# A fused adaLN attention block on one core: key columns from scaled, unshifted rows, modulation one group ahead, gate spread by DMA

## The chip, the cores and the metric

The kernel runs on one NeuronCore of a Trainium2 chip. The metric is the device time of one execution in microseconds (us); a median over runs is given with its range. The profile of a run reports a *span*, from the first to the last instruction.

## The reference

```python
B, N, D = 2, 256, 1152
mod = (silu(c) @ w_mod).reshape(B, 6, 1, D)
shift_a, scale_a, gate_a = mod[:, 0], mod[:, 1], mod[:, 2]     # the other three are not used
h   = layernorm(x) * (1 + scale_a) + shift_a
q, k, v = split(h @ wqkv)                                      # each [B, N, D]
p   = softmax(q @ k^T * D**-0.5)
out = x + gate_a * ((p @ v) @ wo)
```

All tensors are bf16. One fact makes the change legal. The shift adds the same vector to every row of `h`, so it adds the same vector `s` to every key. A score then gets the extra term `q . s`, which is the same for all keys of one query, and softmax does not see it. Keys may therefore be made from rows without the shift; queries and values may not.

## The kernel before: what the argument touches

The 512 token rows are four tiles of 128 rows (tiles 0 and 1 are batch 0, tiles 2 and 3 batch 1). The 1152 features are nine rows of 128 (index `cc` or `k`). Each row tile is normalized, transposed on TensorE, and then scaled and shifted ("modulated") per feature, which gives `hT`. Scale and shift are computed on TensorE by matmuls with two moving columns, in four groups of features, as their weights arrive.

```python
GROUPS = [(0, 2), (2, 5), (5, 7), (7, 9)]
PASSES = [list(range(0, 7)), list(range(7, 14)), list(range(14, 18))]   # q: columns 0-8, k: 9-17

for g, (a, b_) in enumerate(GROUPS):          # loads, in this order, on one queue
    dma_mod(g)                                # scale weights, then shift weights of the group
    dma_wq(a, b_, 0, 7 * P, wkeys(0, a, b_))  # first seven projection columns
# ... then the other projection columns, the value columns, gate weights, wo

# first projection pass: seven accumulators, features outermost
for g, (a, b_) in enumerate(GROUPS):
    if g > 0:
        mod_mm(g, 1)                          # scale matmuls (128x2)
        mod_mm(g, 0)                          # shift matmuls
        mod_ev(g)                             # PSUM -> SBUF, VectorE
        for cc in range(a, b_):
            for b in range(B):
                modulate(cc, b, ...)          # hT = xnT * (1 + scale) + shift
    for k in range(a, b_):
        for j, bank in zip(PASSES[0], PASS1_BANKS):
            qk_mm(0, j, k, bank)              # 128x512 matmul, both batches
# ... two more passes, values, scores, softmax

# gate: one row of four times 288 columns, spread to 128 partitions by matmul
for k in range(DC):
    for j in range(4):
        ... matmul(ps[bank][32*j:32*(j+1), 0:GW], scT_sb[:, k, :], wgate_ap[...])
# ... copied to gaterow_sb; then, for each batch b and quarter j:
        ... matmul(ps[bank][:, 0:GW], sel_sb[:, 2*j + b, :], gaterow_sb[:, :])
        evac(...)                             # to gate_rep
# output tiles: ga = psum * gate_rep;  xo = x + ga;  DMA out
```

TensorE executes its matmuls in program order, so a matmul that waits holds back the matmuls behind it. `warm(n)` issues `n` matmuls of zeros whose result nobody reads, to keep TensorE active at the start.

Of the kernel before, what the change touches and what calls it, by code (L numbers as in the profile page):

```python
# [153 lines left out]
GROUPS = [(0, 2), (2, 5), (5, 7), (7, 9)]  # L154
PASSES = [list(range(0, 7)), list(range(7, 14)), list(range(14, 18))]
PASS1_BANKS = [5, 6, 0, 1, 2, 3, 4]
# [16 lines left out]
def _build(nc, es, x, c, wqkv, wo, w_mod, out):  # L173
# [25 lines left out]
    warm_sb = sb("warm_sb", [P, 512], bf16)  # L199
    c_sb = sb("c_sb", [2, D], bf16)  # L200
# [5 lines left out]
    mod_sb = sb("mod_sb", [P, 2, DC, 2], f32)  # L206
    gaterow_sb = sb("gaterow_sb", [P, GW], bf16)
    stat_sb = sb("stat_sb", [P, TT, 3, 6], f32)
    sums_sb = sb("sums_sb", [P, TT, 2], f32)
    nm2_sb = sb("nm2_sb", [P, TT], f32)  # L210
# [9 lines left out]
    sel_sb = sb("sel_sb", [P, 2 * 4, P], bf16)  # L220
# [7 lines left out]
    wm_off = {}  # L228
    off = 0
    for g, (a, b_) in enumerate(GROUPS):  # L230
        for kind in range(2):
            wm_off[(g, kind)] = off
            off += DC * (b_ - a) * P

    def wm_ap(g, kind):
        w = (GROUPS[g][1] - GROUPS[g][0]) * P
        return bass.AP(wm_sb, wm_off[(g, kind)], [[2 * DC * D, P], [w, DC], [1, w]])

    wgate_ap = bass.AP(wm_sb, 0, [[2 * DC * D, P], [D, DC], [1, D]])
    wo_ap = bass.AP(wm_sb, DC * D, [[2 * DC * D, P], [D, DC], [1, D]])  # L240

    def wm_keys(lo, hi):
        keys = []
        for (g, kind), o in wm_off.items():
            n = DC * (GROUPS[g][1] - GROUPS[g][0]) * P
            if o < hi and o + n > lo:
                keys.append(("wm", g, kind))
        return keys


    op(AC, lambda e: e.dma_start(c_sb[:, :], c[:, :]), w=[("c",)], dma=True)
    for i in range(TT):
        op(SP, lambda e, i=i: e.dma_start(x_sb[:, i, :], x_pi[:, i, :]), w=[("x", i)], dma=True)  # L253

    def dma_mod(g):
        a, b_ = GROUPS[g]
        for kind in (1, 0):
            base = kind * D
            op(SP, lambda e, g=g, kind=kind, lo=base + a * P, hi=base + b_ * P:
               e.dma_start(wm_ap(g, kind), wm_v[:, :, lo:hi]), w=[("wm", g, kind)], dma=True)  # L260

    def dma_wq(k0, k1, c0, c1, keys):
        op(SP, lambda e: e.dma_start(wq_sb[:, k0:k1, c0:c1], wq_v[:, k0:k1, c0:c1]),
           w=keys, dma=True)

    def wkeys(p, k0, k1):
        return [("w", p, k) for k in range(k0, k1)]

    for g, (a, b_) in enumerate(GROUPS):
        dma_mod(g)  # L270
        dma_wq(a, b_, 0, 7 * P, wkeys(0, a, b_))
    for k0 in range(0, DC, 3):
        dma_wq(k0, k0 + 3, 7 * P, 14 * P, wkeys(1, k0, k0 + 3))
    for k0 in range(0, DC, 3):
        dma_wq(k0, k0 + 3, 14 * P, 18 * P, wkeys(2, k0, k0 + 3))
    for k0 in range(0, DC, 3):
        dma_wq(k0, k0 + 3, 2 * D, 3 * D, wkeys(3, k0, k0 + 3))
# [7 lines left out]
    op(POOL, lambda g: g.memset(eps_sb[:, :], EPS_B), w=[("eps",)])  # L285
    op(POOL, lambda g: g.memset(scT_sb[:, :, :], 0.0), w=[("scT",)])
    op(POOL, lambda g: g.memset(sel_sb[:, :, :], 0.0), w=[("sel",)])
    for j in range(4):
        for b in range(2):
            op(POOL, lambda g, j=j, b=b: g.affine_select(  # L290
                out=sel_sb[:, 2 * j + b, :], in_=sel_sb[:, 2 * j + b, :],
                compare_op=ALU.not_equal, fill=1.0, base=-(32 * j + b),
                pattern=[[0, P]], channel_multiplier=1), r=[("sel",)], w=[("sel",)])

    def warm(n):
        for _ in range(n):
            op(PE, lambda pe: pe.matmul(ps[7][:, 0:512], warm_sb[:, 0:P], warm_sb[:, 0:512],  # L297
                                        start=True, stop=True),
               r=[("warm",)], w=[("ps", 7)])


    op(AC, lambda a: a.preload_act_table_set("natural_log_exp_and_others"))
    warm(4)

    def f_cT(pe):
        last = None
        for k in range(DC):
            last = pe.transpose(psb[6][:, 2 * k:2 * k + 2], c_sb[0:2, k * P:(k + 1) * P],
                                ident[0:2, 0:2])
        return last  # L310
    op(PE, f_cT, r=[("c",), ("ident",)], w=[("ps", 6)])
    cT_ps = psb[6][:, 0:2 * DC].rearrange("p (k b) -> p k b", b=2)
    op(DVE, lambda v: v.tensor_copy(cT_sb[:, :, :], cT_ps), r=[("ps", 6)], w=[("cT",)])
    op(AC, lambda a: a.activation(e1_sb[:, :, :], cT_sb[:, :, :], ACT.Exp, scale=-1.0),
       r=[("cT",)], w=[("e1",)])
    warm(8)


    def stats_dve(i):
        for q in range(3):  # L320
            op(DVE, lambda v, q=q: v.bn_stats(stat_sb[:, i, q, :], x_sb[:, i, q * 384:(q + 1) * 384]),
               r=[("x", i)], w=[("stat", i, q)])
        op(DVE, lambda v: v.bn_aggr(mv_sb[:, i, :], stat_sb[:, i, :, :]),
           r=[("stat", i, q) for q in range(3)], w=[("mean", i), ("var", i)])

    def sum_act(i):
        n = 0 if i == 1 else 2
        junk = qkT_sb[:, 3 * n:3 * n + 3, :].rearrange("p a t -> p (a t)")[:, 0:D]
        jk = [("qk", 3 * n + m) for m in range(3)]
        op(AC, lambda a: a.activation(junk, x_sb[:, i, :], ACT.Copy,  # L330
                                      accum_out=sums_sb[:, i, 0:1]),
           r=[("x", i)], w=jk + [("sum", i)])

    def sq_act(i):
        n = 1 if i == 1 else 3
        junk = qkT_sb[:, 3 * n:3 * n + 3, :].rearrange("p a t -> p (a t)")[:, 0:D]
        jk = [("qk", 3 * n + m) for m in range(3)]
        op(AC, lambda a: a.activation(junk, x_sb[:, i, :], ACT.Square,
                                      accum_out=sums_sb[:, i, 1:2]),
           r=[("x", i)], w=jk + [("sq", i)])  # L340

    def stats_act_end(i):
        op(DVE, lambda v: v.tensor_scalar(mv_sb[:, i, 0:1], sums_sb[:, i, 0:1], 1.0 / D, None,
                                          op0=ALU.mult), r=[("sum", i)], w=[("mean", i)])
        op(DVE, lambda v: v.scalar_tensor_tensor(nm2_sb[:, i:i + 1], sums_sb[:, i, 0:1],
                                                 -1.0 / (D * D), sums_sb[:, i, 0:1],
                                                 ALU.mult, ALU.mult),
           r=[("sum", i)], w=[("nm2", i)])
        op(DVE, lambda v: v.scalar_tensor_tensor(mv_sb[:, i, 1:2], sums_sb[:, i, 1:2],
                                                 1.0 / D, nm2_sb[:, i:i + 1],  # L350
                                                 ALU.mult, ALU.add),
           r=[("sq", i), ("nm2", i)], w=[("var", i)])

    def rstd(i):
        op(AC, lambda a: a.activation(lnv_sb[:, i:i + 1], mv_sb[:, i, 1:2], ACT.Ln,
                                      bias=eps_sb[:, 0:1], scale=1.0),
           r=[("var", i), ("eps",)], w=[("lnv", i)])
        op(AC, lambda a: a.activation(rstd_sb[:, i:i + 1], lnv_sb[:, i:i + 1], ACT.Exp, scale=-0.5),
           r=[("lnv", i)], w=[("rstd", i)])

    def xn(i):
        op(DVE, lambda v: v.tensor_scalar(xo_sb[:, i, :], x_sb[:, i, :], mv_sb[:, i, 0:1],  # L362
                                          rstd_sb[:, i:i + 1], op0=ALU.subtract, op1=ALU.mult),
           r=[("x", i), ("mean", i), ("rstd", i)], w=[("xo", i)])

    def xT(i):
        for cc in range(DC):
            bank, half = cc // 2, cc % 2
            op(PE, lambda pe, cc=cc, bank=bank, half=half: pe.transpose(  # L369
                psb[bank][:, half * T + i * P: half * T + (i + 1) * P],  # L370
                xo_sb[:, i, cc * P:(cc + 1) * P], ident[:, :]),
               r=[("xo", i), ("ident",)], w=[("ps", bank)])

    def xT_out(b, eng_of):
        for bank in range(5):
            n = 2 if bank < 4 else 1
            src = psb[bank][:, 0:n * T].rearrange("p (c t) -> p c t", c=n)[:, :, b * NTOK:(b + 1) * NTOK]
            dst = xnT_sb[:, 2 * bank:2 * bank + n, b * NTOK:(b + 1) * NTOK]
            keys = [("xnT", 2 * bank + h, b) for h in range(n)]
# [5 lines left out]

    def mod_mm(g, kind):
        a, b_ = GROUPS[g]
        w = (b_ - a) * P
        for cc in range(a, b_):
            col = (kind * DC + cc) * 2  # L390
            for k in range(DC):
# [278 lines left out]
```

## Time and profile before

| | before |
|---|---|
| runs quoted before the prediction | 110.34, 113.43, 113.9 us |
| all four runs of the first comparison | median 111.89 us (110.04 to 113.9) |
| profiled span | 110.1 us |
| TensorE busy | 99.1 us, 90% of the span |
| first projection matmul, first value matmul | 16.19 us, 61.6 us |

First the page of the kernel before: its span, TensorE's busy time, and three rows of the time slices (40 equal slices; a digit is the busy share in tenths, for PEclk the granted TensorE clock in tenths of full speed).

```profile
span 110.1 us, 1775 instructions
...
PE 99.1 (90%) x735; PEld 56.2 (51%) x735; DVE 43.9 (40%) x125; ACT 26.7 (24%) x61; POOL 4.2 (4%) x17
...
PE   5959459969969699999999999999999999999990
...
PEclk9999955785999999999999999999999999999999
DMA  3999999999999999996299400000000001112222
```

Counting slices from 0, TensorE is close to full from slice 6 on, with three dents (slices 8, 11 and 13); its clock is low in slices 5 to 9; the DMA engines are saturated in slices 1 to 17. To see which of these counts, look at the chain of work that ended last (columns: start us, length us, what):

```profile
3.06 8.22 DMA wm_sb<-in_w_mod_dram
...
16.19 5.29 PE psbank L459 x14
21.47 1.34 PE psbank L392 x54
22.81 0.02 issue
22.84 0.17 DVE mod_sb L401
23.00 0.08 DVE mod_sb L403
23.08 0.03 issue
23.11 0.61 DVE hT_sb L415 x2
23.72 0.05 issue
23.77 6.39 PE psbank L459 x21
...
37.04 24.73 PE psbank L459 x113
61.77 4.39 PE psbank L509 x27
...
86.98 0.49 PE psbank L601 x4
...
89.44 0.49 PE psbank L601 x4
89.93 17.08 PE psbank L620 x108
```

The last DMA wait of the chain ends at 11.28 us. From 16.19 us the chain is TensorE, except for the group starts: between 22.81 and 23.77 us TensorE waits while VectorE evicts scale and shift and modulates the first feature row. The same stop stands before the other two later groups (0.96 us each). Line 601 is the gate spread, 0.98 us. Note also the first 14 projection matmuls: 0.378 us each, while the 113 at 37 us took 0.219 each. The windows view says why (columns: stretch in us, length, TensorE busy, matmuls, granted clock, DMA share, GB/s):

```profile
core 0: us, PE busy (x), PEclk, DMA share, GB/s
16.20:20.40 4.20, 4.20 (x10) 0.50 1.11 334
20.50:23.80 3.30, 2.33 (x60) 1.00 1.14 316
23.90:27.20 3.30, 3.30 (x9) 0.50 1.18 295
27.30:61.60 34.30, 32.37 (x213) 1.00 0.95 340
```

TensorE had half its clock when the projections began, got full clock at 20.45 us, lost it again at 23.87 and had it back from 27.28 us. (A DMA share above 1 means that packets overlap.) Half-clock time inside the projection stream is 4.3 + 3.4 = 7.7 us, about 3.8 us lost.

### The profile page before, as it was taken

Reading aid. Unit: us, or ns where it says so; the run is one execution under the profiler, and the core shown is the slowest. Engines: PE = TensorE matmul, PEld = TensorE weight load, DVE = VectorE, ACT = ScalarE, POOL = GpSimd, SP = SyncE. Lnnn points to the kernel's source line nnn. Section 1 sums busy time; section 2 is a strip of 40 time slices with the busy share of each in tenths; the row PEclk is TensorE's granted clock in tenths of the full one; section 3 lists DMA queues with packets and bytes.
Section 4 is the critical chain, followed back from the end, with each engine's and each line's share of the span. In section 5 each row is a group of like instructions: output and inputs, shape, how many; then the busy total and the mean of one; then the engine's idle time right before and its main releaser. Section 6 shows DMA issues by size and latency. Waiting matters only on the chain.

```text
span 110.1 us, 1775 instructions
## 1 busy us (share of the span) xinstructions
PE 99.1 (90%) x735; PEld 56.2 (51%) x735; DVE 43.9 (40%) x125; ACT 26.7 (24%) x61; POOL 4.2 (4%) x17
## 2 busy tenths in 40 slices
PE   5959459969969699999999999999999999999990
PEld 1407333533445334444444568766666875655570
DVE  0798570040030380000800422643422785666672
ACT  4579230030020250000500415461111870000000
POOL 6610000000000000000000000000000000000000
PEclk9999955785999999999999999999999999999999
DMA  3999999999999999996299400000000001112222
GB/s 77 323 309 321 333 332 348 292 329 294 369 382 363 366 390 389 396 392 232 20 361 408 176 0 0 6 3 0 0 0 0 6 0 33 56 54 70 71 77 71
DMA packets 18956, 21.06 MB, mean 191 GB/s; under 512 B 770, under 2 KB 14978, under 8 KB 18948
## 3 DMA queue, kind: packets, MB, share of 16 engines
q1 hardware_dynamic: 18944, 20.94, 58.7%
q8 instruction: 6, 0.10, 0.4%
q14 instruction: 2, 0.02, 0.1%
q10 hardware_dynamic: 4, 0.00, 0.0%
HBM read 19.76 MB, written 1.18 MB: 190 GB/s over the span
## 4 chain that ended last, share of the span: by engine, by line
PE 81%; DMA 7%; DVE 6%; SPq 2%; issue 1%; ACT 0%
PE psbank L459 36%; PE psbank L509 16%; PE psbank L620 16%; DMA wm_sb<-in_w_mod_dram 7%; PE psbank L585 4%; PE psbank L522 4%; PE psbank L392 3%; DVE hT_sb L415 2%; SPq L253 2%; PE psbank L572 1%; DVE xnT_sb L381 1%; PE psbank L601 1%; DVE mod_sb L401 1%; DVE ga_sb L627 1%; DVE xo_sb L362 1%
## 5 line engine op out<-in xcount | busy, mean ns | idle before, releaser
L459 PE MATMUL psbank<-hT_sb,wq_sb 128*128 128x512 bf16 x162 | 39.6, 408 | 3.5 <-DVE hT_sb L415 3.5
L459 PEld LDWEIGHTS psbank<-hT_sb,wq_sb 128*128 128x128 bf16 x162 | 16.3, 104 | 25.4 <-issue 5.1
L509 PE MATMUL psbank<-wq_sb,hT_sb 128*128 128x384 bf16 x108 | 18.0, 326 | 0.0
L620 PE MATMUL psbank<-wm_sb,pvT_sb 128*128 128x384 bf16 (+2 forms) x117 | 17.7, 314 | 0.0
L620 PEld LDWEIGHTS psbank<-wm_sb,pvT_sb 128*128 128x128 bf16 x117 | 11.1, 98 | 6.6
L509 PEld LDWEIGHTS psbank<-wq_sb,hT_sb 128*128 128x128 bf16 x108 | 10.5, 98 | 6.9
L466 DVE CAST qkT_sb<-psbank 128x512 bf16<-128x512 f32 x10 | 6.3, 684 | 18.9 <-PE psbank L459 18.9
L468 ACT ACTIVATE qkT_sb<-psbank 128x512 bf16<-128x512 f32 x8 | 4.2, 597 | 21.2 <-PE psbank L459 21.2
L627 DVE TENSOR_TENSOR ga_sb<-psbank,gate_rep 128x384 bf16<-128x384 f32 (+2 forms) x13 | 6.8, 526 | 5.9 <-PE psbank L620 5.9
L297 PE MATMUL psbank<-warm_sb 128*128 128x512 bf16 x17 | 6.9, 556 | 1.2 <-DVE warm_sb L280 1.2
L401 DVE TENSOR_SCALAR mod_sb<-psbank 128x4 f32<-128x4 f32 (+1 forms) x4 | 0.7, 164 | 17.7 <-PE psbank L392 17.7
L417 ACT ACTIVATE hT_sb<-xnT_sb,mod_sb 128x256 bf16<-128x256 bf16 x4 | 2.3, 596 | 18.6 <-DVE mod_sb L403 18.6
L466 DVE CAST v_sb<-psbank 128x384 bf16<-128x384 f32 x6 | 3.2, 555 | 7.7 <-PE psbank L509 7.7
L369 PE MATMUL psbank<-ident,xo_sb 128*128 128x128 bf16 x36 | 3.1, 242 | 3.4 <-DVE xo_sb L362 3.4
L468 ACT ACTIVATE v_sb<-psbank 128x384 bf16<-128x384 f32 x6 | 2.9, 486 | 10.3 <-PE psbank L509 10.3
L392 PEld LDWEIGHTS psbank<-scT_sb,wm_sb 128*128 128x128 bf16 x162 | 4.7, 96 | 1.3 <-DMA wm_sb<-in_w_mod_dram 0.3
L392 PE MATMUL psbank<-scT_sb,wm_sb 128*128 128x2 bf16 x162 | 4.8, 164 | 0.2 <-DMA wm_sb<-in_w_mod_dram 0.2
L369 PEld LDWEIGHTS psbank<-ident,xo_sb 128*128 128x128 bf16 x36 | 2.5, 108 | 4.7 <-DVE xo_sb L362 4.5
L630 DVE TENSOR_TENSOR xo_sb<-x_sb,ga_sb 128x384 bf16<-128x384 bf16 (+2 forms) x13 | 4.5, 342 | 0.4
L585 PE MATMUL psbank<-pT_sb,v_sb 128*128 128x256 bf16 x36 | 4.3, 273 | 0.0
L522 PE MATMUL psbank<-qkT_sb 128*128 128x256 bf16 x36 | 4.1, 273 | 0.0
L415 DVE TENSOR_SCALAR hT_sb<-xnT_sb,mod_sb 128x256 bf16<-128x256 bf16 x14 | 4.0, 342 | 0.1
(57 smaller groups left out, 59.0 us busy)
## 6 DMA issues: line engine op xcount, KB each, us to landing
wm_sb<-in_w_mod_dram SPq DMA_DIRECT2D x6, 576.0 KB, 8.3
wq_sb<-in_wqkv_dram SPq DMA_DIRECT2D x4, 672.0 KB, 8.6
wq_sb<-in_wqkv_dram SPq DMA_DIRECT2D x3, 864.0 KB, 11.1
wm_sb<-in_w_mod_dram SPq DMA_DIRECT2D x1, 2592.0 KB, 17.8
wm_sb<-in_wo_dram SPq DMA_DIRECT2D x1, 2592.0 KB, 9.2
wm_sb<-in_w_mod_dram SPq DMA_DIRECT2D x2, 864.0 KB, 8.9
wq_sb<-in_wqkv_dram SPq DMA_DIRECT2D x3, 448.0 KB, 8.3
x_sb<-in_x_dram SPq DMA_DIRECT2D x4, 288.0 KB, 3.6
```

What stands on the lines that cost most here:

```text
L297: op(PE, lambda pe: pe.matmul(ps[7][:, 0:512], warm_sb[:, 0:P], warm_sb[:, 0:512], start=True, stop=True), r=[("warm",)], w=[("ps", 7)])
L369: op(PE, lambda pe, cc=cc, bank=bank, half=half: pe.transpose(psb[bank][:, half * T + i * P: half * T + (i + 1) * P], xo_sb[:, i, cc * P:( ...
L392: op(PE, lambda pe, cc=cc, k=k, col=col, src=wm_ap(g, kind), lo=(cc - a) * P: pe.matmul(ps[7][:, col:col + 2], src[:, k, lo:lo + P], scT_s ...
L415: op(DVE, lambda v: v.tensor_scalar(dst, src, sc, sh, op0=ALU.mult, op1=ALU.add), r=rk, w=wk)
L459: op(PE, lambda pe: pe.matmul(ps[bank][:, lo:hi], wq_sb[:, k, j * P:(j + 1) * P], hT_sb[:, k, lo:hi], start=(k == 0), stop=(k == DC - 1)), ...
L466: op(DVE, lambda v: v.tensor_copy(dst, src), r=r, w=w)
L468: op(AC, lambda a: a.activation(dst, src, ACT.Copy), r=r, w=w)
L509: op(PE, lambda pe, k=k, q=q, bank=bank: pe.matmul(ps[bank][:, 0:384], hT_sb[:, k, i * P:(i + 1) * P], wq_sb[:, k, 2 * D + q * 384:2 * D + ...
L522: op(PE, lambda pe, cc=cc: pe.matmul(ps[bank][:, 0:NTOK], qkT_sb[:, cc, i * P:(i + 1) * P], qkT_sb[:, DC + cc, b * NTOK:(b + 1) * NTOK], s ...
L585: op(PE, lambda pe, h=h, cc=cc, sbk=sbk: pe.matmul(ps[bank][:, h * NTOK:(h + 1) * NTOK], v_sb[:, 2 * b + sbk, cc * P:(cc + 1) * P], pT_sb[ ...
L620: op(PE, lambda pe, i=i, k=k, c0=c0, c1=c1, n=n, bank=bank: pe.matmul(ps[bank][:, 0:n], pvT_sb[:, k, i * P:(i + 1) * P], wo_ap[:, k, c0:c1 ...
L627: op(DVE, lambda v, b=b, c0=c0, c1=c1, n=n, bank=bank, s=s: v.tensor_tensor(ga_sb[:, s, 0:n], ps[bank][:, 0:n], gate_rep[:, b, c0:c1], ALU ...
```

## The change

There are five parts:

1. Key columns are made first, from scaled but unshifted rows (`h0T`). Scale weights are loaded first, in four groups. The shift weights come later and are added to `h0T` in a second pass, ahead of the query columns. Values use shifted rows.
2. A group's scale matmuls and scaling are issued one group ahead, behind the first seven matmuls of the group in progress. The shift is one group ahead likewise.
3. The work on row tiles is reordered at the start: a third of a tile's statistics goes to ScalarE, small arithmetic to GpSimd, and ten half-width matmuls of batch 0 (five key columns, two feature rows) start before batch 1's rows exist.
4. The gate row is computed earlier and spread by eight DMAs, not by matmuls.
5. GpSimd takes part of the scaling and shifting.

The edit also moves the idle matmuls: the kernel before has 4 and 8 of them at the start and 3 and 2 between the first transposes; the changed kernel has 5 and 9 at the start and none later.

The diff, cut to its core:

```diff
-GROUPS = [(0, 2), (2, 5), (5, 7), (7, 9)]
+SGROUPS = [(0, 2), (2, 4), (4, 6), (6, 9)]
+HGROUPS = [(0, 3), (3, 6), (6, 9)]
+NA = 7
+EARLY = 5
@@ loads
-    for g, (a, b_) in enumerate(GROUPS):
-        dma_mod(g)
-        dma_wq(a, b_, 0, 7 * P, wkeys(0, a, b_))
+    for g, (a, b_) in enumerate(SGROUPS):
+        load_s(g)                                   # scale weights
+        load_w("ka", a, b_, D, D + NA * P)          # seven key columns
+    load_h(0)                                       # shift weights
+    load_w("kb", 0, DC, D + NA * P, 2 * D)
+    for g, (a, b_) in enumerate(HGROUPS):
+        if g:
+            load_h(g)
+        load_w("qa", a, b_, 0, NA * P)
@@ start (cut: statistics, evictions)
+    for k in range(2):
+        for j in range(EARLY):
+            qk_mm("ka", h0T_sb, "pv", DC + j, k, j, b=0, start=(k == 0))
@@ first pass
-    for g, (a, b_) in enumerate(GROUPS):
-        if g > 0:
-            mod_mm(g, 1)
-            mod_mm(g, 0)
-            mod_ev(g)
-            for cc in range(a, b_): ...modulate...
-        for k in range(a, b_):
-            for j, bank in zip(PASSES[0], PASS1_BANKS):
-                qk_mm(0, j, k, bank)
+    for g in range(1, len(SGROUPS)):
+        a, b_ = SGROUPS[g]
+        for k in range(a, b_):
+            for j in range(NA):
+                qk_mm("ka", h0T_sb, "pv", DC + j, k, j)
+            if k == a and g + 1 < len(SGROUPS):
+                s_mm(g + 1)
+                scale_group(g + 1)
+            if k == DC - 2:
+                h_mm(0)
@@ gate
-            op(PE, lambda pe, ...: pe.matmul(ps[bank][:, 0:GW], sel_sb[:, 2 * j + b, :], gaterow_sb[:, :], ...
-            evac(AC if j % 2 == 0 else DVE, gate_rep[:, b, j * GW:(j + 1) * GW], ...
+            row = bass.AP(gaterow_sb, (32 * j + b) * GW, [[GW, 1], [0, P], [1, GW]])
+            op(SP, lambda e, ...: e.dma_start(gate_rep[:, b, j * GW:(j + 1) * GW], row), ...
```

## The prediction

> **What bounds it now.** Busy times by engine: TensorE works 99.1 of 110.1 us, 90%, and it ends 81% of the chain of waits. From the first projection matmul (16.19 us) to the last matmul (107.0) it is the pacemaker; DMA is saturated until about 51 us (330 to 390 GB/s in the slices), but the chain's last DMA wait ends at 11.28 us. So only TensorE time counts after 16 us. The chain, from 16.19 to the end of the q/k projections at 61.77 (45.6 us), holds:
> - 162 matmuls of 128x512: 35.4 us at full rate (113 of them took 24.73 us, 0.219 each);
> - 126 modulation matmuls: 3.1 us;
> - three stops before groups 2 to 4 (modulation evictions, then the first row): 0.96 us each, 2.9 us;
> - lost clock. The first 14 matmuls took 5.29 us, the next 21 took 6.39: 4.0 us over full rate. The granted clock reads 0.50 from 13.7 to 20.5 and from 23.9 to 27.3 us.
> The remaining 45.3 us of TensorE hold 0.98 us of gate broadcast matmuls.
>
> **What changes.**
> 1. Key columns use scaled, unshifted rows; softmax ignores the constant. So before a matmul only a scale is needed, and scales are computed a group ahead, while the previous group multiplies (7 matmuls, 1.5 us, against 0.17 + 2x0.3 on VectorE). I expect all three stops to go: -2.9 us. The modulation matmuls themselves stay.
> 2. The shift is a second pass over h (18 tile halves, 0.3 us each on VectorE, a third on GpSimd). It hides behind the two late key columns (18 x 0.219 = 3.9 us, against about 2.7 us of evictions and 0.6 us of shifts) and behind the query pass: 0.
> 3. Eight broadcast matmuls become DMAs issued after the gate row, more than 10 us before their use: -1.0 us.
> 4. Start. Ten half-width matmuls (batch 0, 1.1 us at full rate) run at about 11 to 13 us. But adding durations along each engine's order, row tile 3 is not sooner: its ScalarE third sits behind tile 2's rstd, which sits behind the scale eviction; its transpose waits for tile 1's evictions. I get batch 1's first matmul at about 17.5 us, 1.3 later than now. Net about +0.2.
> 5. Clock. The Trainium skill, "TensorE: Matmul & The Clock Gate", Part 1, says a free-running window of about 3.4 us of activity decides the clock. The trace agrees: its changes (6.85, 13.7, 20.5, 23.9, 27.3 us) lie on a grid of 3.41. Today the stop at 21.5 to 23.8 lets it fall again. The changed stream has no such stop, so one ramp remains, with 1.5 to 3.4 us lost by phase: about -1.6 against this trace. The two runs near 113.5 are, I think, worse phases (35 matmuls all at half clock lose 7.5 us, 3.5 more than here), so the median gains more.
>
> Sum: 110.1 - 2.9 - 1.0 + 0.2 - 1.6 = **about 105.0 us**, range 102.5 to 108.5. Chances: faster 0.90, same 0.07, slower 0.03.
>
> **What would show it.** Projections end near 56.5 instead of 61.8; no idle over 0.3 us before k/q matmuls after 20 us; one fall of the clock after the warm-up and one rise by 24.5; from the first value matmul to the end about 1 us shorter; less spread between runs. If step 4 is wrong, the first full-width matmul comes far from 19 us.
>
> **What would make it wrong.** GpSimd scales or shifts much slower than 0.5 us, or held up by VectorE; batch 1's rows later than 18.5 us; two extra falls of the clock; a weight load arriving late because keys' loads are reordered; gate copies delaying the outputs.

## The result, and the profile after

The changed kernel took 105.31 us (median of four runs, 104.89 to 106.4), the kernel before 111.89 us (110.04 to 113.9). The ratio is 0.9538, 95% interval 0.9451 to 0.9625. Ratios are the mean time of one kernel's fast runs over that of the other's of the same rounds, so they are not quite the ratio of the medians.

The page of the changed kernel, the same rows:

```profile
span 103.4 us, 1795 instructions
...
PE 94.3 (91%) x728; PEld 55.8 (54%) x734; DVE 44.8 (43%) x122; ACT 25.2 (24%) x64; POOL 8.7 (8%) x30
...
PE   5956458999999999999999999999999999999990
...
PEclk9999985579999999999999999999999999999999
DMA  2999999999999999999999400002777666764122
```

The three dents are gone. There is one low stretch of clock in place of two. The DMA row has something new: about 0.6 to 0.7 in slices 28 to 35, where before there was nothing until the outputs. Its chain (line 367 is the modulation matmuls, 419 the projections, 579 the values, 660 and 685 the attention output and `wo`):

```profile
3.16 5.87 DMA wm_sb<-in_w_mod_dram
...
13.98 1.20 PE psbank L349 x17
...
16.01 2.31 PE psbank L419 x10
18.32 0.22 issue
18.54 3.90 PE psbank L419 x10
22.44 0.43 PE psbank L367 x18
22.87 3.04 PE psbank L419 x14
...
55.86 4.55 PE psbank L579 x27
...
79.28 3.93 PE psbank L660 x36
83.20 17.08 PE psbank L685 x108
```

From 18.54 us there is no link on VectorE or GpSimd between TensorE's pieces: modulation matmuls (22.44) are followed at once by projections (22.87). The 0.22 us of "issue" before 18.54 is no stop but a lost record: the page lists 728 matmuls for 734 weight loads, one of these loads stands at 18.12 us without its matmul, and the full trace of after_again (734 of 734) has no such gap. The clock in windows:

```profile
core 0: us, PE busy (x), PEclk, DMA share, GB/s
10.50:14.80 4.30, 2.07 (x25) 1.00 1.13 325
15.00:21.60 6.60, 6.10 (x39) 0.50 1.08 347
21.80:55.80 34.00, 33.74 (x265) 1.00 1.08 366
```

The span fell by 6.7 us. The first value matmul came 5.75 us sooner (61.61 to 55.86 us), and from there to the end of the last `wo` matmul the time fell from 45.9 to 44.9 us. In the first part, the stops account for 2.9 us (2.90 to none), the ten early half-width matmuls for 1.1 us (five full ones at 0.2155 us each), the earlier first matmul of the stream for 0.2 us, and the clock for 1.0 us (half-clock time in the stream 7.7 to 5.7 us). That is 5.2 of 5.75 us; about 0.6 us is not itemised here.

Last, the new DMA work, from the view of the tile that the gate copies write:

```profile
L646 SPq DMA_DIRECT2D gate_rep<-gaterow_sb x8: 542/2264/3380, 70.4 to 84.4; - x8
...
DMA to landing us min/median/max: 5.4/8.7/11.1
```

Eight copies of only 72 KB each were issued over 14 us (the issue itself took up to 3.4 us), and each landed 5.4 to 11.1 us after it was issued. From the trace's landing times, the first four (batch 0) landed at 75.9 to 83.9 us and the others (batch 1) at 87.2 to 92.6 us; batch 0's gate is first used at 84.7 us. Together they moved 590 KB in 22.1 us, 27 GB/s, where the loads of the first half ran at over 300. The first output write could only be issued at 87.1 us, behind them on the same queue, and landed at 92.9 us. Nothing on the chain waited for this. The least slack was 3.6 us: the quarter of batch 1's gate that landed at 91.3 us is first read at 94.9 us.

### The profile page after: what moved, and what is told of

Read it like the earlier page. It is cut to its first block, busy times and chain, and to the rows that moved or that the text cites. A ratio compares the mean times of both kernels' runs of the same rounds, so it can differ in the third digit from the quotient of the medians.

```text
span 103.4 us, 1795 instructions
## 1 busy us (share of the span) xinstructions
PE 94.3 (91%) x728; PEld 55.8 (54%) x734; DVE 44.8 (43%) x122; ACT 25.2 (24%) x64; POOL 8.7 (8%) x30
## 4 chain that ended last, share of the span: by engine, by line
PE 83%; DMA 6%; DVE 3%; ACT 2%; SPq 2%; issue 1%; POOL 0%; POOLq 0%
PE psbank L419 35%; PE psbank L579 17%; PE psbank L685 17%; DMA wm_sb<-in_w_mod_dram 6%; PE psbank L592 4%; PE psbank L660 4%; PE psbank L367 4%; SPq L252 2%; PE psbank L637 1%; PE psbank L349 1%; DVE pvT_sb L399 1%; DVE ga_sb L692 1%; ACT lnv_sb L334 1%; DVE xo_sb L695 0%; ACT junk_sb L314 0%
## 5 line engine op out<-in xcount | busy, mean ns | idle before, releaser
L419 PE MATMUL psbank<-pvT_sb,wq_sb 128*128 128x512 bf16 (+1 forms) x88 | 20.6, 393 | 1.4 <-DVE pvT_sb L399 1.0
L419 PE MATMUL psbank<-hT_sb,wq_sb 128*128 128x512 bf16 x78 | 17.5, 379 | 0.1
L419 PEld LDWEIGHTS psbank<-pvT_sb,wq_sb 128*128 128x128 bf16 x91 | 9.5, 108 | 10.7 <-issue 2.4
L579 PEld LDWEIGHTS psbank<-wq_sb,hT_sb 128*128 128x128 bf16 x108 | 10.5, 98 | 7.0 <-issue 0.2
L419 PEld LDWEIGHTS psbank<-hT_sb,wq_sb 128*128 128x128 bf16 x81 | 7.8, 98 | 9.1
L294 PE MATMUL psbank<-warm_sb 128*128 128x512 bf16 x14 | 4.9, 506 | 1.2 <-DVE warm_sb L283 1.2
L349 PE MATMUL psbank<-ident,xo_sb 128*128 128x128 bf16 x36 | 2.6, 225 | 3.4 <-ACT xnT_sb L302 2.2
L387 DVE COPY sh_sb<-psbank 128x6 f32<-128x6 f32 x3 | 0.5, 165 | 11.3 <-PE psbank L367 11.3
L306 DVE BATCH_NORM_STATS2 stat_sb<-x_sb 128x6 f32<-128x384 bf16 x9 | 4.5, 535 | 0.0
L378 DVE TENSOR_SCALAR s_sb<-psbank 128x4 f32<-128x4 f32 (+1 forms) x4 | 0.6, 160 | 8.8 <-PE psbank L367 8.8
L413 POOL TENSOR_SCALAR hT_sb<-pvT_sb,sh_sb 128x256 bf16<-128x256 bf16 x6 | 3.2, 533 | 14.8 <-DVE sh_sb L387 14.8
## 6 DMA issues: line engine op xcount, KB each, us to landing
wq_sb<-in_wqkv_dram SPq DMA_DIRECT2D x4, 672.0 KB, 10.6
```

The costliest lines, as they stand in the source:

```text
L294: op(PE, lambda pe: pe.matmul(ps[bank][:, 0:512], warm_sb[:, 0:P], warm_sb[:, 0:512], start=True, stop=True), r=[("warm",)], w=[("ps", bank)])
L306: op(DVE, lambda v: v.bn_stats(stat_sb[:, i, 2 * q:2 * q + 2, :].rearrange("p a b -> p (a b)"), x_sb[:, i, q * 384:(q + 1) * 384]), r=[("x ...
L419: op(PE, lambda pe: pe.matmul(ps[bank][:, lo:hi], wq_sb[:, k, col * P:(col + 1) * P], src[:, k, lo:hi], start=(k == 0) if start is None el ...
L579: op(PE, lambda pe, k=k, q=q, bank=bank: pe.matmul(ps[bank][:, 0:384], hT_sb[:, k, i * P:(i + 1) * P], wq_sb[:, k, 2 * D + q * 384:2 * D + ...
```

## The experiments

Three sets of kernels ran, each set on one chip together with the kernel before. That kernel's medians there were 112.53, 111.98 and 112.33 us (11 runs each), so medians of different sets can be compared to within about 0.5 us. A run is marked slow here when it is over 1.5% above the fastest run of its kernel in its set. Ratios use fast runs alone; medians use all.

| run | set | median us (range), runs | ratio to before (95%) |
|---|---|---|---|
| after_again | 1 | 105.66 (105.17 to 107.46), 6 | 0.9388 (0.9336 to 0.9439) |
| undo_gate_dma | 1 | 107.24 (106.4 to 107.89), 6 | 0.9514 (0.946 to 0.9569) |
| undo_ahead | 1 | 107.5 (106.17 to 107.69), 6 | 0.9533 (0.9478 to 0.9589) |
| before_ahead | 1 | 107.87 (106.11 to 109.15), 6 | 0.9483 (0.9392 to 0.9575) |
| undo_early | 2 | 107.19 (106.45 to 108.36), 6 | none |
| fill_gap | 2 | 103.65 (102.3 to 104.47), 6 | none |
| tile3_sooner | 2 | 102.16 (100.53 to 104.02), 6 | none |
| gate_late | 2 | 111.03 (109.96 to 111.73), 4 | none |
| after_third | 3 | 105.62 (104.76 to 106.56), 6 | 0.9421 (0.9359 to 0.9483) |
| tile3_fill | 3 | 101.51 (101.06 to 103.47), 6 | 0.9061 (0.9004 to 0.9118) |
| before_ahead_gate | 3 | 107.73 (107.46 to 108.55), 6 | 0.9639 (0.9585 to 0.9693) |
| gate_src_spread | 3 | 106.28, 1 | none |

In the second set one run of the kernel before took 107.82 us, which made its other ten runs count as slow, so no ratio was formed; medians are used. That run is worth a look: its granted clock was 0.998, so the kernel before with hardly any half clock took 107.8 us, 4 us less than its median. All results were correct except gate_src_spread, which is wrong on purpose.

### after_again and after_third: the reference

No edit.

> The changed kernel once more, unedited, as the reference for the runs beside it. Expected 104.9 to 106.4 us (the four runs so far), ratio to before 0.94 to 0.96. The clock theory says that the runs differ only by where the activity window falls: span and mean granted clock of its runs should go together (higher clock, shorter span), and the same for the kernel before, with a larger spread there (110.0 to 113.9 so far).

> The changed kernel unedited, as the reference on this chip: 105 to 106.5 us.

Measured: 105.66 and 105.62 us on two chips, as expected (one run of 107.46 us was above the range, and the ratio of 0.9388 a little below it). The clock row of the first profile:

```profile
PEclk9999555599999999999999999999999999999999
```

This profile shows how much the clock's timing varies: half clock from 10.6 to 20.8 us, where the first trace of the changed kernel had it from 14.9 to 21.7 us. Batch 1's first matmul came at 17.5 us in place of 16.0, and yet the spans are 103.7 and 103.4 us: the late start was bought back by an earlier end of the half clock. The expected tie of higher mean clock to shorter span held over the 16 runs of the changed kernel: six at 0.965 to 0.967 had spans of 103.0 to 103.6 us, ten at 0.948 to 0.952 had 103.4 to 105.7. It is not strict (the first four alone had 103.4 us both at 0.967 and at 0.951), because half clock hurts only where TensorE has work to do: of 6.8 us of half clock in the first trace 5.7 lay in the stream, of 10.2 us in this one only 3.3.

### undo_ahead: the scale matmuls back at the start of their group

```diff
+        if g > 1:
+            s_mm(g)
+            scale_group(g)
         for k in range(a, b_):
             ...
-            if k == a and g + 1 < len(SGROUPS):
-                s_mm(g + 1)
-                scale_group(g + 1)
```

> The changed kernel with the scale matmuls of groups 3 and 4 and their scaling put back to the start of their own group, nothing else. Theory: each of the two group starts shows a stop of 0.7 to 0.9 us (eviction 0.17, then a tile half 0.3 on VectorE and 0.56 on GpSimd), so 1.4 to 1.8 us slower than after_again, more if the clock falls at a stop. Rival, the matmuls of other columns or the clock window absorb it: under 0.5 us.

Measured: 107.5 us, 1.84 us slower than after_again by medians and 1.6 us by the ratios, whose intervals are 0.6 us wide to each side. TensorE's waits, from the waits view (what waited, for whom; us in total, times, longest):

```profile
PE psbank L419 <- POOL pvT_sb L401: 1.8, 2, 0.9
```

Two waits for the last-finished half of a feature row, 0.92 us each, are the two stops that the edit puts back, and the time rose by about their sum. (The traced run is the fastest of the six, 106.17 us; its stream began at 16.34 us where that of after_again's trace began at 17.54, which hides part of the price in that one trace.) So the issue order alone makes or removes a stop, and a stop costs about its length.

### before_ahead: the order without unshifted keys

This is the rival to the title of the change: perhaps the keys have little to do with it. The edit moves the whole modulation of the next group, scale and shift, ahead by one feature row in the kernel before, with no change to loads or keys.

```diff
     for g, (a, b_) in enumerate(GROUPS):
-        if g > 0:
-            mod_mm(g, 1); mod_mm(g, 0); mod_ev(g); ...modulate...
         for k in range(a, b_):
             for j, bank in zip(PASSES[0], PASS1_BANKS):
                 qk_mm(0, j, k, bank)
+            if k == b_ - 2 and g + 1 < len(GROUPS):
+                mod_group(g + 1)      # the same calls as were removed above
```

> The kernel before with only one edit: scale and shift matmuls, eviction and modulation of a group one row of seven matmuls before the previous group ends; DMA order and keys as before. Theory that the stops and the second fall of the clock are what the change removed, and that unshifted keys are only the means: idle before the projection matmuls falls from 2.9 us to under 0.5, the clock falls once, 3.5 to 5 us faster than before (ratio 0.955 to 0.97). Rival, that the shift weights land too late for this without the new load order (18.2, 24.1, 29.3 us): at least 0.5 us of stop remains at each group and the gain is under 2 us.

Measured: 107.87 us, 4.66 us faster than before on the same chip, of the changed kernel's 6.87, by medians. Only two of the six runs are fast (106.11 and 107.34 us); by the ratios of fast runs it is 0.0517 of 0.0612, five sixths of the gain. TensorE's waits:

```profile
PE psbank L459 <- DVE hT_sb L415: 0.9, 1, 0.9
PE psbank L392 <- DMA wm_sb<-in_w_mod_dram: 0.3, 1, 0.3
```

The first is the wait for the very first rows, not a group start. The second is the only price of loading shift weights early, 0.35 us, once. The stops are gone and the clock fell once (half clock from 16.5 to 23.3 us). So two thirds to five sixths of the gain came from issuing modulation ahead, which needed neither unshifted keys nor a new load order. The rival of this run, that the shift weights land too late, is refuted.

### undo_gate_dma: the gate spread by TensorE again

```diff
-            row = bass.AP(gaterow_sb, ...)
-            op(SP, ... e.dma_start(gate_rep[...], row), ...)
+        for j in range(4):           # after each batch's pv matmuls
+            op(PE, ... pe.matmul(ps[bank][:, 0:GW], sel_sb[:, 2 * j + b, :], gaterow_sb[:, :], ...))
+            evac(AC if j % 2 == 0 else DVE, gate_rep[...], ps[bank][:, 0:GW], ...)
```

The cut leaves out nine GpSimd instructions that make the selection matrix `sel_sb`, which are put back too.

> The changed kernel with the gate rows spread by eight TensorE matmuls again (0.98 us of TensorE in the trace of before) instead of eight DMAs. Theory: this term was worth its TensorE time, so 0.8 to 1.1 us slower than after_again (ratio about 0.009 higher), all of it between the first value matmul and the end. Rival: the slow DMAs (landing 5 to 11 us after issue, output writes held back to 92.9 us) give some of it back, then it is under 0.4 us slower, or faster.

Measured: 107.24 us, 1.58 us slower than after_again (about 1.4 us by the ratios, whose intervals are 0.6 us wide to each side), more than the expected 0.8 to 1.1; the rival (under 0.4 us) is refuted. In the traces, first value matmul to last `wo` matmul takes 45.9 us in every profiled kernel with the matmul spread and 44.9 us in every profiled kernel with the DMA spread, whatever came before. The term is 0.98 us. Of the other 0.4 to 0.6 us a part lies outside the span: the median spans differ by 1.25 us (105.1 and 103.85), and this run's times are 2.1 to 2.3 us longer than its spans, after_again's 1.8 to 1.9. Why is not known.

### gate_late and gate_src_spread: how near the copies came to being late

gate_late moves the gate row and its copies behind the last value tile:

```diff
     v_tile(1)
-    <gate row matmuls, gaterow copy, eight DMAs>
     v_tile(2)
     p_T(0)
     p_T(1)
     v_tile(3)
+    <gate row matmuls, gaterow copy, eight DMAs>
```

> The changed kernel with the gate row and its eight DMAs where the kernel before has the row, after the last value tile (about 79 us instead of 69). In the changed kernel the eight copies landed 75.9 to 92.6 us, 22 us after the first was issued, while batch 1's gate is first used at 93.5. Theory that the copies are slow and have about 1 us to spare: 10 us later they stop the outputs, 3 to 5 us slower, with VectorE's gate products waiting on DMA. Rival, that they were only slow because nothing waited for them or other traffic was ahead: under 1 us.

Measured: 111.03 us, 5.4 us slower than the changed kernel, which eats most of the whole gain. VectorE's waits:

```profile
DVE ga_sb L692 <- DMA gate_rep<-gaterow_sb: 10.6, 6, 4.1
```

The copies were issued from 80.7 us and landed from 86.1 to 102.6 us, again 22 us from first issue to last landing. The expected 3 to 5 us was slightly exceeded. (The expectation's "about 1 us to spare" compares different quarters of the gate; by quarter the least slack was 3.6 us, and copies that land 10 us later overrun it by about 6 us.) So the DMA spread pays only together with the earlier place of the gate row.

gate_src_spread keeps size, number and place, but reads 128 different partitions of a tile of zeros in place of one partition 128 times:

```diff
-            row = bass.AP(gaterow_sb, (32 * j + b) * GW, [[GW, 1], [0, P], [1, GW]])
+            row = warm_sb[:, 0:GW]
```

> Wrong result on purpose: the changed kernel with the eight gate copies reading 128 different partitions of a tile of zeros instead of one partition over and over; same sizes, count and place. Theory that reading one partition 128 times is what makes the copies slow (72 KB landing 5.4 to 11.1 us after issue, the last 22 us after the first issue): here each lands within 3 us of its issue, all eight within 6 us. Rival, that their short rows (576 bytes) or SBUF to SBUF copies are slow as such: landing as before.

The view of the tile that they write:

```profile
L646 SPq DMA_DIRECT2D gate_rep<-warm_sb x8: 515/601/608, 71.5 to 75.9; - x8
...
DMA to landing us min/median/max: 1.9/1.9/2.0
```

All eight landed within 6.4 us of the first issue (expected: 6). The trace has the same 1024 packets of 576 bytes, at a mean of 29 ns each in place of 220. So neither the size nor the short rows nor the SBUF-to-SBUF path is slow; reading one partition over and over is. The Trainium skill, "DMA: Bandwidth & Descriptors", Specifications, asks for at least 512 bytes per transfer for full rate; the 576-byte rows are above that, and this run agrees that they are not the problem. Each copy moved 72 KB in a median of 8.7 us against 1.9. This rests on one run, but each of its eight copies shows it; its time, 106.28 us, lies within after_third's range, as it should if nothing waited for the copies.

### undo_early: no half-width matmuls

```diff
-    for k in range(2):
-        for j in range(EARLY):
-            qk_mm("ka", h0T_sb, "pv", DC + j, k, j, b=0, start=(k == 0))
     ...
     for k in range(2):
-        for j in range(EARLY):
-            qk_mm("ka", h0T_sb, "pv", DC + j, k, j, b=1, start=False)
-    for k in range(2):
-        for j in range(EARLY, NA):
+        for j in range(NA):
             qk_mm("ka", h0T_sb, "pv", DC + j, k, j)
```

> The changed kernel without the ten early half-width matmuls of batch 0: all key columns start full width when both batches are scaled. Theory: those ten are TensorE work moved into idle time, worth their own length, 1.1 us at full clock, so 0.9 to 1.4 us slower than the changed kernel (ratio about 0.010 higher). Rival: at half clock they only fill what the transposes then lose, or their activity moves the clock's window; then under 0.5 us slower, or faster.

Measured: 107.19 us, 1.5 us above the changed kernel's 105.6 to 105.7 on other chips, a little more than the work's own 1.1 us. By median spans it is 1.2 us (105.05 against 103.85 and 103.8); the rest lies outside the span, as two of its six runs are 2.3 and 2.8 us longer than their spans. The rival (under 0.5 us) is refuted.

### fill_gap: idle matmuls against the fall of the clock

```diff
-EARLY = 5
+EARLY = 4
 ...
             qk_mm("ka", h0T_sb, "pv", DC + j, k, j, b=0, start=(k == 0))
+    warm(8)
```

> The changed kernel with eight idle matmuls (128x512 of zeros) in the gap after the early matmuls (about 11.8 to 13.9 us), in a bank set free by taking one column less early (worth 0.2 us). Theory that TensorE activity in a 3.4 us window decides the clock: the fall at 10.6 to 14.9 us goes in some runs, and the half-clock time inside the projection stream (3.3 and 5.7 us in the two traces so far) shrinks; 0.5 to 2 us faster than the changed kernel at the median. Rival: the clock falls anyway, then the fill runs at half speed and pushes the transposes back: 0.5 to 1.5 us slower.

Measured: 103.65 us, 2.0 us faster than the changed kernel, although it does slightly more work. The windows view of its profile:

```profile
10.50:15.60 5.10, 4.37 (x52) 1.00 1.11 335
15.70:52.90 37.20, 37.20 (x288) 1.00 1.08 360
```

Full clock throughout, and the first value matmul at 53.0 us against 55.9. The profile fell on the fastest of its six runs; the record has the granted clock of the others: 1.0 in the three runs from 102.3 to 103.37 us, 0.983 in the three from 103.92 to 104.47. This is the direct test of the clock term of the prediction: adding useless TensorE work before the stream shortened the kernel by about what half clock had cost. Against after_again's trace the first value matmul is 3.24 us sooner: 1.65 us are half clock inside the stream (3.3 us of it), 1.85 us are the stream's earlier start (15.69 in place of 17.54 us), and 0.2 us is lost with the early column.

### tile3_sooner: batch 1's rows earlier

The same instructions; on VectorE and ScalarE those of row tile 3 move up.

```diff
     xT_out(0, 0, AC)
+    third_act(3)
     xT_out(1, 0, DVE)
+    bn(3, 0)
+    third_end(3)
     s_ev(0)
     scale_x(0, 0, DVE)
     scale_x(1, 0, DVE)
     aggr(2, True)
     rstd(2)
-    third_act(3)
-    bn(3, 0)
-    xn(2)
     bn(3, 1)
-    third_end(3)
     aggr(3, True)
-    rstd(3)
+    xn(2)
     xT_out(0, 1, AC)
-    xn(3)
-    xT_out(1, 1, DVE)
+    rstd(3)
     xT_last(0, AC)
+    xT_out(1, 1, DVE)
+    xn(3)
```

> The changed kernel with the same instructions, those of row tile 3 moved up on VectorE and ScalarE: its ScalarE third before tile 2's rstd, its statistics before tile 2's normalization, tile 1's evictions before tile 3's normalization. Theory of the prediction's step 4, that batch 1 is late because of this order: batch 1's first matmul comes 1 to 2 us sooner (16.0 and 17.5 us in the two traces so far, here 14 to 15.8) and the kernel is 1 to 2 us faster (ratio 0.009 to 0.018 lower). Rival: the clock, not the order, sets the start; then under 0.5 us.

Measured: 102.16 us, 3.5 us faster, more than either theory allowed. The one profile (a run of 102.44 us, against the kernel's fastest of 100.53) does not show the expected path: batch 1's first matmul came at 16.0 us, no sooner, but half clock lasted only from 11.4 to 14.8 us and was over before the stream began, as its clock row shows:

```profile
PEclk9999759999999999999999999999999999999998
```

So the order matters, but in that trace through the clock, by leaving TensorE fewer idle moments, and not through an earlier start. The two fastest runs, 100.53 and 100.55 us, were not traced, but the record gives them a granted clock of 1.0. fill_gap at the same clock took 102.3 to 103.4 us, so about 2 to 3 us look like the order's own (an estimate, between kernels that also differ in the fill and one early column). How the gain divides between order and clock stays open.

### tile3_fill: both

The edit of tile3_sooner, four early columns in place of five, and eight idle matmuls in five gaps before the stream: two after tile 0's transposes, two after the first scale matmuls, two after the early matmuls, one between the transposes of tiles 2 and 3, and one after the second scale matmuls. (The expectation says nine; that was a miscount.)

```diff
     xT(0)
+    warm(2)
     xT(1)
     s_mm(0)
+    warm(2)
 ... early matmuls
+    warm(2)
     xT(2)
+    warm(1)
     xT(3)
     s_mm(1)
+    warm(1)
```

> The version that the experiments point to: row tile 3's work moved up (102.2 us alone) plus nine idle matmuls in five small gaps of TensorE before the projection stream (8 in one gap gave 103.7 alone). Theory: the order sets when the stream can start, the fill keeps the clock up, so the two add in part: 100.5 to 101.8 us, no or little half-clock time between 10 us and the end of the projections, less spread than tile3_sooner (100.5 to 104.0). Rival: the fill delays transposes that are now close together, then 102 us or more.

Measured: 101.51 us (101.06 to 103.47), in the expected range. All six runs are below the lowest of after_third on the same chip (104.76). In its profile the clock was full from 6.2 us to past the last matmul, and the first value matmul came at 52.9 us:

```profile
PEclk9999999999999999999999999999999999999999
```

This version beats both kernels: 4.1 us below the changed one, ratio to before 0.9061. Whether it beats tile3_sooner is not shown: tile3_sooner's two runs at full clock (100.5 us) are faster than the five here (101.06 to 102.26), but only two of its six runs kept that clock, where here five did and the sixth had 0.983. On this record the fill buys steadiness.

### before_ahead_gate: what is left for unshifted keys

before_ahead with the gate row moved up and spread by DMA as in the changed kernel.

```diff
     v_tile(1)
+    <gate row matmuls, gaterow copy, eight DMAs>
     v_tile(2)
 ...
-            op(PE, ... pe.matmul(ps[bank][:, 0:GW], sel_sb[:, 2 * j + b, :], gaterow_sb[:, :], ...))
-            evac(...)
```

The cut leaves out that the nine GpSimd instructions for `sel_sb` go away with it.

> The kernel before with modulation one group ahead (107.9 us alone) and the gate by DMA, as in the changed kernel; keys still from shifted rows. Theory: the two terms add, 106.5 to 107.2 us, and what is left to the changed kernel (105 to 106.5) is the early start, 1 to 1.5 us: unshifted keys themselves buy only that. Rival: unshifted keys with the new load order carry more; then this stays above 107.5.

Measured: 107.73 us, against 107.87 us for before_ahead in another set: the expected 1 us did not appear, and the time is above the theory's range. In the profile the gate's term is there (value start to last matmul 44.9 us instead of 45.9), but the start gave it back: half clock from 7.8 to 21.4 us, the first projection matmul at 18.5 us instead of 15.8. Its clock row:

```profile
PEclk9995555599999999999999999999999999999999
```

The other five runs lost their time the same way, as far as the record goes: all six have a granted clock of 0.935 or 0.936, those of before_ahead 0.935 to 0.984. In the trace the clock had risen sooner than in before_ahead's (4.4 in place of 6.3 us), the idle matmuls of the start ended sooner (5.7 in place of 6.7), and TensorE then stood idle for 2.9 us in place of 1.75 before the first transposes; what set this off was not tested. So the sum of the two terms failed here, and what unshifted keys are worth by themselves, somewhere between nothing and 2 us, stays open. What can be said is that they permit the early half-width matmuls as soon as the scale alone is known (they start at 10.5 us, while before the shift weights of the first group landed only at 11.3 us), and that these are worth 1.1 to 1.5 us. Even this may not need them: in the trace of before, batch 0's first two shifted rows and their weights were ready at 12.84 us, and TensorE stood idle until 14.39. Such a kernel was not run, and it would need other PSUM banks for its transposes.

## Why the prediction was right, and where it was not

The predicted 105.0 us was measured as 105.31 us, and faster by over 2% was right. The agreement of 0.3 us is better than the reasoning: two errors cancel, which is luck. The base is about 1.9 us too low, and the gain was forecast 1.4 us too small.

| term | predicted | measured | by |
|---|---|---|---|
| three stops | -2.9 | -2.9 | trace; undo_ahead: two stops put back cost 1.84 |
| shift pass | 0 | 0: no stop before a query matmul | trace of after_again, which has all its records |
| gate spread | -1.0 | -0.98 | traces; timed 1.4 to 1.6 in undo_gate_dma |
| start | +0.2 | -1.3 in the first trace, +0.3 in after_again | first projection matmul of the stream 16.19 to 16.01 and to 17.54, minus 1.1 of early work |
| clock | -1.6 | -1.0 in the first trace, -2.2 in after_again | half-clock time in the stream 7.7 to 5.7 and 3.3 us |
| sum, spans | -5.3 | -6.7 | 110.1 to 103.4; the terms above give -6.2, and about 0.6 us is not itemised |
| span to time | left out | +1.9 | 105.28 against 103.4 |

- **The base was wrong.** The sum starts from 110.1, which is a span, and its result was given as a time. The 110.1 us span belongs to a run of about 112 us (an estimate: the span plus the 1.7 to 2.8 us seen in the other runs), in the middle of the kernel's range, not to its best run as the prediction took it. The reading that the runs near 113.5 us lost 3.5 us more than the trace falls with it: they are about 1.5 us above it.
- **The stops** were read correctly: in the changed trace no projection matmul after 18.54 us waits, and undo_ahead shows that the order is the cause. But the prediction credited the unshifted keys ("only a scale is needed") along with the order. before_ahead shows that the order alone is enough, scale and shift together: 4.66 of 6.87 us by medians, five sixths by fast runs.
- **The gate** was right in size. "More than 10 us before their use" was right of the issue and said nothing of the landing: the copies take 22 us in all, the least slack was 3.6 us, and gate_late shows what it costs to overrun it. The prediction named "gate copies delaying the outputs" as a risk; early outputs were delayed, from which nothing followed, since the last ones were not.
- **The start is the mis-sized term.** "Batch 1's first matmul at about 17.5 us" came true in after_again (17.5) and not in the first trace (16.0); it depends on whether the transposes run at half clock. The net of +0.2 us was wrong in the first trace by 1.5 us and right in after_again (+0.3); undo_early shows the early work to be worth 1.5 us in time, 1.2 us in spans.
- **The clock** term was right in kind and in size on average. "One fall of the clock after the warm-up and one rise by 24.5" holds in both traces (rises at 21.7 and 20.8 us), and fill_gap shows directly that keeping full clock is worth 2 us at the median. That is more than the stream alone (1.65 us against after_again's trace): half clock before the stream also made it start late, which the prediction did not count. The Trainium skill, "TensorE: Matmul & The Clock Gate", Part 1, describes a free-running window of about 3.4 us; all changes in the traces lie on a grid of 3.41 us, as in the trace of before: 13.63, 20.45, 23.87, 27.28 us.
- **GpSimd** was not a problem: a tile half took it 0.48 us while VectorE was not at such work, against 0.28 us on VectorE alone. Where both worked at once GpSimd took 0.55 to 0.57 us, and 7 of VectorE's 15 instructions took 0.42 to 0.51. The Trainium skill, "GPSIMD Engine Reference", section 3, has 1.96 times VectorE's time for an fp32 add of two inputs; for these bf16 operations of one input it is 1.7 here, each engine alone, and the work was hidden.

## What to carry to other kernels

When an in-order engine stops at a group boundary for a small result, first try to issue that result's work one step ahead; here this alone gave two thirds to five sixths of the gain, and the algebra that seemed to make it possible was not needed for it. Count clock as a resource: eight idle matmuls in the gap before a long matmul stream bought 2 us, and reordering small work so that TensorE idles less there bought 3.5, part of it perhaps by the order itself. A broadcast by DMA from one partition frees the engine but takes several times longer than its bytes suggest, so give it a long lead, and never add a span to a time.

## What the Trainium skill lacked or had wrong

- "TensorE: Matmul & The Clock Gate", "Why this matters for your kernels", advises no TensorE idle gap over about 3 us between bursts to keep the clock. That is too lenient here: in the kernel before the clock fell at 23.87 us, at the end of a 3.41 us window in which TensorE was busy for 2.33 of 3.3 us and the longest gap was 0.97 us; 54 of its 60 matmuls there were of two columns. A gap of that length is not enough by itself: the other two stops of before (0.96 us each) and the two of undo_ahead (0.92) cost no clock. Filling a gap of about 2 us (fill_gap) kept the clock at 1.0 in three of six runs and at 0.983 in the others.
- "DMA: Bandwidth & Descriptors" has no figure for how long an issue takes behind slow copies on its queue: here up to 3.4 us behind copies that read one SBUF partition 128 times, against 0.6 us behind copies that read 128 partitions.
- No page that I looked up gives the offset between a profile's span, from the first to the last instruction, and the timed figure: 1.7 to 2.8 us in the runs here.
